# Reordering the start of a fused adaLN, attention and feed-forward kernel: token tiles on one queue, head columns copied earlier, zero matmuls moved, one row task moved

## The chip, the cores and the metric

The kernel runs on one core of one Trainium2 chip. The metric is the device time of one execution in microseconds (us). "Before" is the tuned kernel. In the profile PE is TensorE, PEld its weight loads, DVE is VectorE, ACT is ScalarE, POOL is GpSimd, SP is the sync engine that issues most DMAs. Times within an execution count from the start of the profiled span.

## The reference

One transformer block: layer norm with a conditioning shift and gain, attention over the last 512 positions of a cache, output projection, a second layer norm, and a gated feed-forward part.

```python
mod = (_silu(c) @ w_mod).reshape(c.shape[0], 6, 1, -1)
sa, ca, ga, sb, cb, gb = (mod[:, i] for i in range(6))         # abridged
h = _layernorm(x) * (1 + ca) + sa
x = x + ga * _A_ref(h, A_k_cache, A_v_cache, A_wq, A_wo)       # 32 heads, 4 kv heads, width 128
h = _layernorm(x) * (1 + cb) + sb
x = x + gb * _B_ref(h, B_w_gate, B_w_up, B_w_down)             # silu(x Wg) * (x Wu) @ Wd
```

There are 2048 tokens of width 1024, worked on in four chunks of 512, each of four tiles of 128 tokens.

## The kernel before

A small tracker (`T.op`) emits each instruction and puts a semaphore wait before it for every buffer it reads or writes. `warm(n, b)` issues n matmuls of zeros (128x128 by 128x512) into PSUM bank b; they compute nothing. The parts that matter are the head (the first 30 us), where TensorE waits for data, and one background task.

The head loads the four token tiles on two DMA queues, and SP goes on to the conditioning weights:

```python
for t in range(TPC):
    q = Q_xa[t // 2] if t % 2 else Q_x[t]
    T.op(q, lambda: (A if t % 2 else SP).dma_start(x_res[:, t, :], xf[t * P:(t + 1) * P, :]), writes=[B_x[t]])
```

Then each tile is normalized (statistics on DVE for three tiles, on ACT for the fourth), transposed on TensorE, and, between the transposes, the gain (`mod_ca`) is computed with one-column matmuls:

```python
warm(8, WB)
x_first(0)                       # 8 transposes, wait for DVE's norm(0)
warm(4, WB)
x_first(1)
for k in range(3):
    mod_ca(k)
    warm(1, WB)
x_first(2)
# ... mod_ca(3..7), x_first(3), single zero matmuls between ...
warm(4, WB)
x_mod()                          # gain read from PSUM, hT = transposed x * gain
```

The query projection of the first four heads starts from hT without the shift; the shift's own product (`mod_sa`) is still on its way. It is added later as a bias column for each head (the "bias products", one-column matmuls into bank SCB + 2):

```python
mod_sa(2)
mod_sa(3)
# ... DVE copies the shift out of PSUM; k_turn(0): transposes of the first keys ...
warm(2, SCB + 3)
# 32 one-column bias products for 4 heads
warm(3, SCB + 3)
# ... shift(0..4) on DVE and ACT ...
q_out(0)                         # DVE: query of head 0 + its column, read from PSUM
T.op(DVE, lambda: V.tensor_copy(bq[:, :], psap((SCB + 2) * 512, [[2, LEAD + 1]])), ...)   # columns to SBUF
q_out(2, True)                   # ACT, needs bq
q_out(3, True)
# shift(5..7) on DVE, q_out(1)
```

In the main loop, background tasks are Python generators in a list; each iteration runs one step of the first. `row_task` spreads a row over all partitions: POOL builds diagonal matrices, TensorE multiplies them by ones into bank XB, DVE casts the bank (line 588). Bank XB is also one of the two banks of the output projection, which comes after the last head of each chunk.

```python
if i == 31:
    bg.insert(0, row_task(sc_row, B_scr, sc_bf[:, :], B_sc))
```

The softmax here doesn't subtract the row's maximum and nothing guards it: scores larger than these inputs give would overflow.

## Time and profile before

| | before |
|---|---|
| time, three runs | 1281.66 us median, 1280.07 to 1282.6 |
| span of the profile | 1280.4 us (this execution took 1282.21 us) |
| TensorE on the chain that ended last | 99% |
| all waits of TensorE's matmuls | 7.0 us |
| clock below full after the first release | 3.4 us at half |

The chain line of the page says that everything hangs on TensorE:

```profile
PE 99%; DMA 1%; DVE 0%; ACT 0%; POOL 0%; ACTq 0%; issue 0%; DVEq 0%
```

Since TensorE is the chain, only two things can make the kernel faster without doing less: idle time of TensorE and its clock. The view of the waits, for PE (who waited, for whom: us in total, times, longest), lists its idle time up to its last matmul:

```profile
PE ps L268 <- POOL arena L391: 2.2, 1, 2.2
PE ps L268 <- DVE arena L588: 1.9, 1, 1.9
PE ps L268 <- DVE arena L656: 1.4, 1, 1.4
PE ps L272 <- DVE nsc L409: 0.8, 2, 0.4
PE ps L268 <- DVE arena L470: 0.4, 1, 0.4
PE ps L272 <- DVE arena L409: 0.3, 1, 0.3
```

Line 588 is the cast of the row task; it stands at 155.7 us, inside the output projection. The timeline there (start, duration, instruction, and in brackets the idle time before it with its releaser):

```profile
154.40 0.69 DVE L734 TENSOR_TENSOR tmp<-ps,rowb 128x512 f32<-128x512 f32 x1 [6.00 <-PE ps L268]
155.13 0.69 DVE L736 TENSOR_TENSOR x_res<-tmp,x_res 128x512 bf16<-128x512 f32 x1
155.74 0.68 DVE L588 CAST arena<-ps 128x512 bf16<-128x512 f32 x1
...
156.48 1.68 PE L268 MATMUL ps<-arena 128*128 128x512 bf16 x7 [1.89 <-DVE arena L588]
```

The cast queues behind the two residual operations of the first output block, and the second output block needs the bank that the cast reads.

The table of windows gives the granted clock of TensorE (the number after the five engines' busy times and counts):

```profile
27.00:28.00 1.00, 0.00 (x0) 0.00 (x0) 0.96 (x5) 0.66 (x2) 0.00 (x0) 0.97 1.21 313
28.00:29.00 1.00, 0.91 (x3) 0.36 (x4) 0.76 (x2) 0.61 (x2) 0.00 (x0) 0.50 0.87 195
29.00:30.00 1.00, 1.00 (x4) 0.37 (x3) 0.00 (x0) 0.84 (x1) 0.00 (x0) 0.50 0.71 134
30.00:31.00 1.00, 1.00 (x3) 0.30 (x2) 0.00 (x0) 0.91 (x2) 0.00 (x0) 0.50 0.85 237
31.00:32.00 1.00, 1.00 (x5) 0.45 (x4) 0.00 (x0) 0.30 (x1) 0.00 (x0) 0.82 1.08 386
```

For 3.4 us the clock is at half. And the timeline of PE alone shows pieces of the head (four lines out of some thirty):

```profile
7.24 0.71 PE L272 MATMUL ps<-arena,nsc 128*128 128x128 bf16 x8 [0.40 <-DVE nsc L409]
7.79 1.03 PE L268 MATMUL ps<-arena 128*128 128x512 bf16 x4
...
15.65 3.83 PE L268 MATMUL ps<-arena 128*128 128x512 bf16 x16 [0.43 <-DVE arena L470]
...
28.09 4.36 PE L268 MATMUL ps<-arena 128*128 128x512 bf16 x12 [1.38 <-DVE arena L656]
```

They are the first transposes, the zero matmuls after them, the first query matmul at 15.65 us and the first scores at 28.09 us.

### The profile page before, as it was taken

What the parts mean: (1) busy time and instruction counts of PE and PEld (TensorE: products, weight loads), DVE (VectorE), ACT (ScalarE), POOL (GpSimd) and SP (SyncE); (2) the same over time, 40 slices, a digit from 0 to 9 for tenths busy, and PEclk for the clock granted to TensorE, in tenths of its full rate; (3) what the DMA queues carried; (4) which work ended last, traced back from release to release, by engine and by line L of the source; (5) the groups of instructions that cost most, each with busy time, mean ns of one, the idle gap of its engine ahead of it and who ended that gap; (6) DMA issues with size and microseconds to landing.
All of it is one profiled execution on the core that took longest, in us unless ns stands there. A gap on an engine that the chain in (4) does not pass through costs nothing.

```text
span 1280.4 us, 17849 instructions
## 1 busy us (share of the span) xinstructions
PE 1270.6 (99%) x7651; PEld 645.0 (50%) x7651; DVE 477.3 (37%) x884; ACT 339.8 (27%) x384; POOL 41.8 (3%) x102
## 2 busy tenths in 40 slices
PE   8999999999999999999999999999999999999999
PEld 4565545555455564455554444444444444444444
DVE  3555314765137652265422331233222331221222
ACT  3555303555015551055520111011100111011100
POOL 1011000000000010000000000000000000000000
PEclk9999999999999999999999999999999999999999
DMA  9999402966008841055352974046421654035200
GB/s 317 226 242 239 104 1 50 214 141 158 16 17 171 170 105 42 1 128 112 73 150 68 289 234 132 17 142 170 132 74 39 199 150 132 17 112 168 67 9 25
DMA packets 234830, 155.31 MB, mean 121 GB/s; under 512 B 129024, under 2 KB 220032, under 8 KB 234752
## 3 DMA queue, kind: packets, MB, share of 16 engines
q1 hardware_dynamic: 176208, 94.93, 30.8%
q10 hardware_dynamic: 58544, 59.25, 14.7%
q8 instruction: 60, 0.98, 0.3%
q14 instruction: 18, 0.15, 0.0%
HBM read 119.54 MB, written 4.19 MB: 97 GB/s over the span
## 4 chain that ended last, share of the span: by engine, by line
PE 99%; DMA 1%; DVE 0%; ACT 0%; POOL 0%; ACTq 0%; issue 0%; DVEq 0%
PE ps L268 98%; DMA x_res<-in_A_x_dram 1%; PE ps L272 0%; ACT arena L490 0%; DVE tmp L734 0%; DVE arena L656 0%; DVE arena L661 0%; DVE x_res L736 0%; DVE arena L588 0%; ACTq L305 0%; POOL rstd L499 0%; DVE arena L409 0%; DVE arena L736 0%; DVE arena L470 0%; ACTq L308 0%
## 5 line engine op out<-in xcount | busy, mean ns | idle before, releaser
L268 PE MATMUL ps<-arena 128*128 128x512 bf16 (+1 forms) x7378 | 1265.4, 334 | 5.9 <-POOL arena L391 2.2
L268 PEld LDWEIGHTS ps<-arena 128*128 128x128 bf16 x7378 | 635.9, 98 | 624.7 <-issue 5.2
L694 ACT ACTIVATE arena<-ps 128x1024 bf16<-128x1024 f32 x256 | 261.9, 1023 | 358.4 <-PE ps L268 346.7
L919 ACT ACTIVATE arena<-ps 128x512 bf16<-128x512 f32 x112 | 66.9, 597 | 506.5 <-PE ps L268 506.5
L920 DVE TENSOR_TENSOR arena<-ps,arena 128x512 bf16<-128x512 f32 x112 | 77.5, 692 | 276.2 <-PE ps L268 276.2
L734 DVE TENSOR_TENSOR tmp<-ps,rowb 128x512 f32<-128x512 f32 (+1 forms) x65 | 44.4, 683 | 320.8 <-PE ps L268 320.8
L611 DVE CAST arena<-ps 128x512 bf16<-128x512 f32 x124 | 85.8, 692 | 59.7 <-PE ps L268 59.7
L715 DVE TENSOR_TENSOR arena<-ps,rl 128x512 bf16<-128x512 f32 x128 | 88.5, 691 | 4.7 <-DVE rl L712 0.2
L712 DVE RECIPROCAL rl<-ps 128x4 f32<-128x4 f32 x128 | 23.4, 182 | 120.5 <-PE ps L268 120.5
L398 DVE BATCH_NORM_STATS2 st<-x_res 128x6 f32<-128x512 bf16 x62 | 42.4, 683 | 3.7 <-DMA x_res<-in_A_x_dram 3.6
L403 POOL TENSOR_SCALAR rstd<-mv 128x1 f32<-128x1 f32 x28 | 6.2, 221 | 883.5 <-DVE mv L402 883.5
L565 DVE SCALAR_TENSOR_TENSOR arena<-arena 128x1024 bf16<-128x1024 bf16 x24 | 29.2, 1216 | 0.0
L736 DVE TENSOR_TENSOR arena<-tmp,x_res 128x512 bf16<-128x512 f32 (+1 forms) x33 | 22.3, 676 | 1.1
L736 DVE TENSOR_TENSOR x_res<-tmp,x_res 128x512 bf16<-128x512 f32 x32 | 22.1, 692 | 1.1
L414 DVE TENSOR_SCALAR arena<-arena,gain,mod_bf 128x512 bf16<-128x512 bf16 x56 | 20.4, 406 | 0.0
L409 DVE TENSOR_SCALAR nsc<-x_res,mv,rstd 128x1024 bf16<-128x1024 bf16 x30 | 16.0, 534 | 0.0
L580 POOL TENSOR_SCALAR arena<-arena,c 128x128 bf16<-128x128 bf16 x24 | 14.4, 616 | 46.7 <-PE ps L268 46.4
L405 POOL TENSOR_TENSOR rstd<-rstd,mhalf 128x1 f32<-128x1 f32 x28 | 15.8, 564 | 2.3
L268 PEld LDWEIGHTS ps<-sc_bf,arena 128*128 128x128 bf16 x192 | 7.2, 96 | 3.2
L268 PE MATMUL ps<-sc_bf,arena 128*128 128x1 bf16 x192 | 7.3, 163 | 0.0
L402 DVE BATCH_NORM_AGGREGATE mv<-st 128x2 f32<-128x12 f32 x28 | 5.8, 209 | 1.0
L272 PE MATMUL ps<-arena 128*128 128x128 bf16 x32 | 2.8, 219 | 0.3 <-DVE arena L409 0.3
(54 smaller groups left out, 40.0 us busy)
## 6 DMA issues: line engine op xcount, KB each, us to landing
arena<-in_A_wq_dram SPq DMA_DIRECT2D x31, 1024.0 KB, 5.6
arena<-in_B_w_gate_dram ACTq DMA_DIRECT2D x28, 1024.0 KB, 5.4
arena<-in_B_w_up_dram ACTq DMA_DIRECT2D x28, 1024.0 KB, 8.2
arena<-in_A_wo_dram SPq DMA_DIRECT2D x8, 1024.0 KB, 7.0
arena<-in_B_w_down_dram SPq DMA_DIRECT2D x7, 1024.0 KB, 8.2
out_dram<-arena SPq DMA_DIRECT2D x15, 256.0 KB, 2.0
x_res<-in_A_x_dram SPq DMA_DIRECT2D x3, 1024.0 KB, 6.6
arena<-in_w_mod_dram SPq DMA_DIRECT2D x8, 256.0 KB, 7.1
```

The costliest lines, as they stand in the source:

```text
L268: T.op(PE, lambda: TE.matmul(out_ap, lhsT, rhs, start=start, stop=stop, skip_group_check=skip), reads=reads, writes=[bank_buf])
L398: T.op(DVE, lambda: V.bn_stats(st_[sl][:, hf * 6:hf * 6 + 6], x_res[:, t, hf * 512:hf * 512 + 512]), reads=[B_x[t]], writes=[B_st[sl]])
L414: T.op(DVE, lambda: V.tensor_scalar(dst[:, dt, :], dst[:, dt, :], gain[gi][:, dt:dt + 1], mod_bf[:, ccol + dt:ccol + dt + 1], op0=ALU.mult ...
L565: T.op(DVE, lambda: V.scalar_tensor_tensor(mt[n % 2], mt[n % 2], 1.0, sc_row, op0=ALU.mult, op1=ALU.mult, accum_out=mcol[:, n:n + 1]), rea ...
L611: T.op(DVE, lambda: V.tensor_copy(qT_s[qs], bank(b)), writes=[PB[b], B_qT[qs]])
L694: T.op(ACT, lambda: A.activation(ex_s[es][:, 2 * kp:2 * kp + 2, :], banks2(SCB + 2 * kp), AF.Exp, scale=att_scale), writes=[PB[SCB + 2 * k ...
L712: T.op(DVE, lambda: V.reciprocal(rl[r][:, :].rearrange("p (a b) -> p a b", a=2), psap(PVB * 512 + P, [[512, 2], [130, 2]])), writes=both + ...
L715: T.op(DVE, lambda: V.tensor_tensor(o_s[os_].rearrange("p (a b) d -> p a b d", a=2), psap(PVB * 512, [[512, 2], [130, 2], [1, P]]), rlb, A ...
L734: T.op(DVE, lambda: V.tensor_tensor(tmp[s][:, 0:n], bank(b, n), rowb[ri][:, c0:c0 + n], ALU.mult), reads=[B_row[ri]], writes=[PB[b], B_tmp ...
L736: T.op(DVE, lambda: V.tensor_tensor(dst[:, c0:c0 + n], tmp[s][:, 0:n], x_res[:, t, c0:c0 + n], ALU.add), reads=[B_tmp[s], B_x[t]], writes= ...
L919: T.op(ACT, lambda: A.activation(sg_s[ss], bank(gb), AF.Silu), writes=[PB[gb], B_sg[ss]])
L920: T.op(DVE, lambda: V.tensor_tensor(guT[:, ft, :], bank(ub), sg_s[ss], ALU.mult), reads=[B_sg[ss]], writes=[PB[ub], B_gu[ft]])
```

## The change

Its intent is to cut idle time of TensorE in the head, to keep its clock up with zero matmuls, and to take the row task out of the output projection. The diff, cut to its core:

```diff
-            Q_xa = [dq("q_xa%d" % i, A) for i in range(2)]
             for t in range(TPC):
-                q = Q_xa[t // 2] if t % 2 else Q_x[t]
-                T.op(q, lambda: (A if t % 2 else SP).dma_start(x_res[:, t, :], ...), writes=[B_x[t]])
+                T.op(Q_x[t], lambda: SP.dma_start(x_res[:, t, :], ...), writes=[B_x[t]])
 ...
-                T.op(DVE, lambda: V.tensor_copy(gain_f[:, :], gain[0][:, :]), ...)
+                T.op(ACT, lambda: A.activation(gain_f[:, :], gain[0][:, :], AF.Copy), ...)
 ...
-            warm(8, WB)
+            warm(7, WB)
             x_first(0)
-            warm(4, WB)
+            warm(5, WB)
             x_first(1)
 ...
             mod_sa(2)
+            warm(2, SCB + 3)
             mod_sa(3)
 ...
-            warm(2, SCB + 3)
+            warm(3, SCB + 3)
             # bias products
-            warm(3, SCB + 3)
+            warm(5, SCB + 3)
 ...
             # q_out: head 0 no longer reads its column from PSUM, but from bq as the others do
+            T.op(DVE, lambda: V.tensor_copy(bq[:, :], psap(...)), writes=[PB[SCB + 2], B_bq])
             q_out(0)
-            T.op(DVE, lambda: V.tensor_copy(bq[:, :], psap(...)), writes=[PB[SCB + 2], B_bq])
             q_out(2, True)
 ...
-                if i == 31:
-                    bg.insert(0, row_task(sc_row, B_scr, sc_bf[:, :], B_sc))
+                if i == 17:
+                    bg.append(row_task(sc_row, B_scr, sc_bf[:, :], B_sc))
```

More of the change, by code (lines that the diff above doesn't have):

```diff
@@ L302, in load_x @@
                      writes=B_x[ch * TPC:(ch + 1) * TPC])
-            Q_xa = [dq("q_xa%d" % i, A) for i in range(2)]
             T.op(Q_c, lambda: A.dma_start(c_row[:, :], c.rearrange("o (k p) -> (o k) p", p=P)), writes=[B_cT])
             for t in range(TPC):
-                q = Q_xa[t // 2] if t % 2 else Q_x[t]
-                T.op(q, lambda: (A if t % 2 else SP).dma_start(x_res[:, t, :], xf[t * P:(t + 1) * P, :]), writes=[B_x[t]])
+                T.op(Q_x[t], lambda: SP.dma_start(x_res[:, t, :], xf[t * P:(t + 1) * P, :]), writes=[B_x[t]])
             OFF_WO = 0
@@ L465, in x_mod @@
                 mod_gain(0, 0, DT, B_modc, B_g[0])
-                T.op(DVE, lambda: V.tensor_copy(gain_f[:, :], gain[0][:, :]), reads=[B_g[0]], writes=[B_gf])
+                T.op(ACT, lambda: A.activation(gain_f[:, :], gain[0][:, :], AF.Copy), reads=[B_g[0]], writes=[B_gf])
                 for dt in range(DT):
@@ L659, in q_out @@
             def q_out(h, on_act=False):
-                if h == 0:
-                    T.op(DVE, lambda: V.tensor_scalar(qT_s[h], bank(QB0[h]), bank(SCB + 2, 1, 2 * h), None, op0=ALU.add),
-                         writes=[PB[QB0[h]], PB[SCB + 2], B_qT[h]])
-                elif on_act:
+                if on_act:
                     T.op(ACT, lambda: A.activation(qT_s[h], bank(QB0[h]), AF.Identity, bias=bq[:, h:h + 1]),
@@ L672, in _ @@
             shift(4, True)
+            T.op(DVE, lambda: V.tensor_copy(bq[:, :], psap((SCB + 2) * 512, [[2, LEAD + 1]])), writes=[PB[SCB + 2], B_bq])
             q_out(0)
-            T.op(DVE, lambda: V.tensor_copy(bq[:, :], psap((SCB + 2) * 512, [[2, LEAD + 1]])), writes=[PB[SCB + 2], B_bq])
             q_out(2, True)
```

## The prediction

> **What bounds it.** TensorE. The chain of waits is 99% PE over a span of 1280.4 us. The list of PE's waits holds only 7.0 us in the whole run: 2.2 us for the first memset, 1.9 us for a cast of the row task (DVE, line 588), 1.4 us for the shifts before the first scores, 1.5 us in small waits of the head. Besides, one clock loss: the table of windows shows a granted clock of 0.97 in 27 to 28 us, 0.50 from 28 to 31 us, 0.82 in 31 to 32 us, and 1.00 after. That is about 3.4 us at half speed (the timeline's matmuls start every 0.43 us instead of 0.216), a cost of about 1.7 us. All that can be won lies in some 5 to 8 us.
>
> **Each part, costed.**
>
> 1. Row of conditioning. Its second half now falls behind the first output-projection block (PE idle 154.6 to 156.5 us, behind two residual operations and the cast). Appended behind the second chunk's normalization it should run about iterations 27 to 29, inside the head loop, where the bank is free and DVE has slack: -1.9 us.
>
> 2. Clock gate. PE idles about 1.4 us before 28.09 us, after many one-column matmuls. The Trainium skill, "TensorE: Matmul & The Clock Gate" (Part 1), says the gate halves the clock after an idle window of 3413 ns; the trace agrees in length (3.4 us). Five more zero matmuls (2 before the last shift product, 1 and 2 around the bias products) and a shorter wait should keep the window busy: -1.7 us if it works (75 to 80%); the timed runs of before may not all have it.
>
> 3. Head columns copied first. Before, ACT's query copy of head 2 waits 1.1 us for the column copy, which queues behind head 0's DVE copy (0.76 us); the scores start at 28.09 us when that ACT copy ends. With the 0.16 us column copy first, ACT starts some 0.75 us earlier and the scores some 0.7 us earlier: -0.7 us.
>
> 4. Token tiles on SP. The fourth tile (ACT queue) lands 6.5 us after issue, at 8.2 us; the tiles on SP took about 3 us. It should land near 5.5 us. But PE has its own serial work there: the third transposes can move only from 11.38 to about 10.93 us. So only about -0.45 us reaches PE.
>
> 5. Gain copied on ACT instead of DVE: DVE starts the first multiply 0.17 us earlier: -0.15 us.
>
> 6. Cost of the added zero matmuls: the two before the last shift product delay it (its weights landed before): +0.43 us; the third before the bias products: +0.15 us; the two after fill idle time: 0.
>
> Sum: -1.9 -1.7 -0.7 -0.45 -0.15 +0.6 = -4.3 us. As an expectation with the doubt about the clock: about -4.0 us.
>
> **Predicted time** 1277.4 us, range 1275.3 to 1279.6. Chances: faster by over 2% 0.01, within 2% 0.98, slower by over 2% 0.01.
>
> **What would show it.** The 1.9 us wait on line 588 gone; clock 1.00 all through 25 to 35 us and 0.216 us matmul spacing; the first scores at about 27.3 us (28.1 before); the fourth tile's landing near 5.5 us but the first query matmul at about 15.0 us, not 13 (15.65 before); PE busy time down by about 1.7 us.
>
> **What would make it wrong.** The clock gate still closing, or closing in only some executions of either kernel, as its window runs free: then the gain is nearer 2.5 us. The row task meeting another wait in its new place. The SP queue delaying the conditioning weights (the last landed at about 12.8 us), so that the head waits for them.

## The result, and the profile after

The changed kernel took 1278.87 us in the median of four runs (1277.92, 1278.26, 1279.48, 1279.70); the kernel before took 1281.76 us in the same set (1280.07 to 1282.6). The ratio is 0.9979, with a 95% interval from 0.9962 to 0.9996. A ratio here is the mean time of one kernel's fast runs over that of the other's of the same rounds, so it is not quite the ratio of the medians. By the measure of 2% the two kernels are the same. The span of the profile went from 1280.4 to 1277.9 us; the profiled execution of the changed kernel is the one of 1279.70 us, its slowest.

TensorE's waits in the changed kernel:

```profile
PE ps L268 <- POOL arena L389: 2.2, 1, 2.2
PE ps L272 <- DVE nsc L407: 1.1, 1, 1.1
PE ps L268 <- DVE arena L468: 0.4, 1, 0.4
PE ps L268 <- DVE arena L663: 0.3, 1, 0.3
```

The wait of 1.9 us on the row task's cast is gone, and the wait before the scores fell from 1.4 to 0.3 us. But the wait for DVE's first normalized tile, ahead of the first transposes, is now 1.1 us (0.4 us before). The table of windows no longer shows the clock at half at 28 us:

```profile
28.00:29.00 1.00, 0.90 (x5) 0.19 (x2) 0.82 (x2) 0.65 (x2) 0.00 (x0) 1.00 0.67 149
29.00:30.00 1.00, 0.76 (x4) 0.42 (x5) 1.00 (x5) 0.74 (x3) 0.00 (x0) 1.00 0.61 122
30.00:31.00 1.00, 1.00 (x7) 0.42 (x5) 0.54 (x1) 0.91 (x2) 0.00 (x0) 1.00 0.93 271
```

The same four pieces in the timeline of PE:

```profile
7.51 1.04 PE L272 MATMUL ps<-arena,nsc 128*128 128x128 bf16 x8 [1.10 <-DVE nsc L407]
...
8.34 2.34 PE L268 MATMUL ps<-arena 128*128 128x512 bf16 x5
...
16.77 3.89 PE L268 MATMUL ps<-arena 128*128 128x512 bf16 x16 [0.36 <-DVE arena L468]
...
29.24 2.75 PE L268 MATMUL ps<-arena 128*128 128x512 bf16 x12 [0.35 <-DVE arena L663]
```

Here is a surprise. Five zero matmuls take 2.34 us, where four took 1.03 us before: they ran at half clock, 0.43 us each. The first query matmul starts at 16.77 us, 1.1 us later than before, though I had predicted 0.6 us earlier; the first scores start at 29.24 us, not at 27.3 us as predicted. They then run at full clock: from the scores to the next key transposes are 2.59 us instead of 4.20 us. The trace's record of the clock has its first release at 11.50 us (7.47 us before). The clock column of the windows does not show it: it reads 1.00 from the start, although the zero matmuls at 3 to 6 us take 0.43 us in both kernels. One has to read the spacing of equal matmuls to see the start.

So two profiles stand against each other: before, the clock came up early and fell once; changed, it came up late and never fell. Which of this is the change, and which is luck?

### The profile page after: what moved, and what is told of

It is laid out like the page before. It is cut to its first block, busy times and chain, and to the rows that moved or that the text cites. A ratio compares the mean times of both kernels' runs of the same rounds, so it can differ in the third digit from the quotient of the medians.

```text
span 1277.9 us, 17862 instructions
## 1 busy us (share of the span) xinstructions
PE 1271.0 (99%) x7656; PEld 646.3 (51%) x7656; DVE 477.2 (37%) x883; ACT 340.3 (27%) x385; POOL 42.2 (3%) x102
## 4 chain that ended last, share of the span: by engine, by line
PE 99%; DVE 0%; DMA 0%; ACT 0%; issue 0%; ACTq 0%
PE ps L268 99%; PE ps L272 0%; DMA x_res<-in_A_x_dram 0%; DVE st L396 0%; DVE arena L663 0%; ACT arena L471 0%; DVE arena L468 0%; DVE tmp L730 0%; DVE arena L732 0%; DVE nsc L407 0%; DVE mv L493 0%; DVE gain L448 0%; DVE mod_bf L462 0%; DVE bq L669 0%; ACTq L79 0%
## 5 line engine op out<-in xcount | busy, mean ns | idle before, releaser
L268 PE MATMUL ps<-arena 128*128 128x512 bf16 (+2 forms) x7383 | 1265.7, 334 | 3.0 <-POOL arena L389 2.2
```

Source lines behind the costliest of these rows:

```text
L268: T.op(PE, lambda: TE.matmul(out_ap, lhsT, rhs, start=start, stop=stop, skip_group_check=skip), reads=reads, writes=[bank_buf])
```

## The experiments

Theory A: the clock is decided by how busy TensorE is within windows of fixed length that run free of the kernel's start. The Trainium skill, "TensorE: Matmul & The Clock Gate", Part 1, describes such a window of 3413 ns. The length agrees with the profile before: its record of the clock has the half clock from 27.95 to 31.36 us, 3.41 us, and 20.48 us, six times that, from the first release to the fall. Then both events depend on where the windows happen to lie, and idle time of TensorE makes them likely. Theory B: the late release is a fixed consequence of the edit. The other experiments undo one part each. Times of kernels sent together share the runs of the kernel before: first set 1280.15 us median of nine (one of them above 1281), second set 1280.24 us (four above 1281), third set 1280.09 us (two above 1281). The sets ran on three different chips, but the lowest of each are 1280.05, 1280.08 and 1280.03 us, so the sets can be compared to about 0.1 us; where I compare across sets I say so.

### The changed kernel again (first set)

No edit.

> The changed kernel once more, unedited, for a second profile and more times. Theory A (the clock's first release is decided by how busy TensorE is in a free-running window of about 3.4 us, and the changed kernel leaves TensorE idle 1.1 us before the first transposes, so in some executions the release comes one window late): the release time differs from the 11.5 us of the first profile if the window's phase differs, it lies anywhere in about 5.5 to 12 us, and the times fall in a range of about 1.5 us or more (1277.9 to 1279.7). Theory B (the late release is a fixed consequence of the edit, for instance of the later landing of the first tile): release again at about 11.5 us and times within about 0.5 us of each other. Ratio to before about 0.998 in both.

Measured: 1277.85 us median, 1277.77 to 1277.93 in five runs; ratio 0.998 (0.9968 to 0.9993). The timeline of PE of this execution:

```profile
7.08 0.92 PE L272 MATMUL ps<-arena,nsc 128*128 128x128 bf16 x8 [0.67 <-DVE nsc L407]
7.84 1.24 PE L268 MATMUL ps<-arena 128*128 128x512 bf16 x5
...
14.92 3.89 PE L268 MATMUL ps<-arena 128*128 128x512 bf16 x16 [0.36 <-DVE arena L468]
...
27.39 2.75 PE L268 MATMUL ps<-arena 128*128 128x512 bf16 x12 [0.35 <-DVE arena L663]
```

The same code; the five zero matmuls run at full clock, the first query matmul starts at 14.92 us and the scores at 27.39 us, as predicted (15.0 and 27.3 us). The record of the clock has the release at 7.75 us. So the late release is not fixed by the code. My expectation of a spread of 1.5 us within the set was wrong: all five lie together here. Theory B as I wrote it falls; whether the idle time has a part in it is for the next runs.

### Nine, four and one zero matmuls before the first transposes

```diff
-            warm(7, WB)
+            warm(9, WB)      # a3; a4: warm(4); c0: warm(1)
             x_first(0)
```

> The changed kernel with nine instead of seven zero matmuls before the first transposes, which fills the 1.1 us gap with two cold matmuls of 0.43 us and delays nothing (the transposes wait for the vector engine until 7.5 us). Theory A: the release of the clock comes at 8.1 us or earlier in any phase, the first query matmul at about 15.6 us instead of 16.8 us, and the time falls to about 1277.5 us with a narrower spread. Theory B (phase or tile landing alone, the zero matmuls do not matter): no change against the changed kernel, 1278.9 us, release late as often.

> The changed kernel with four instead of seven zero matmuls before the first transposes: the suspected cost enlarged, TensorE is idle about 2.4 us there. Theory A: release one window late in nearly every phase (11 us or later), all times near or above the slower cluster of the changed kernel, about 1279.6 to 1281 us. Theory B: as the changed kernel, 1278.9 us.

> The changed kernel with one instead of seven zero matmuls before the first transposes, so that TensorE is idle about 3.3 us there, nearly a whole window. Theory A (the release of the clock needs a busy window): released one window late in every execution, zero matmuls of 0.43 us still between the first and second transposes, first query matmul at about 16 us or later (14.9 us in the fast profile of the changed kernel), time 1279.5 us or more in all runs. Theory B: no change, 1277.9 us.

Measured: nine, 1277.88 us (1277.85 to 1277.99, five runs). Four, 1279.58 us median: one run at 1277.78, the others 1279.11 to 1279.86. One (second set), 1279.73 us, 1278.83 to 1280.09 in four runs, released at 11.59 us and with the zero matmuls after the first transposes at half clock:

```profile
7.11 1.04 PE L272 MATMUL ps<-arena,nsc 128*128 128x128 bf16 x8 [3.26 <-DVE nsc L407]
7.94 2.34 PE L268 MATMUL ps<-arena 128*128 128x512 bf16 x5
...
16.56 3.89 PE L268 MATMUL ps<-arena 128*128 128x512 bf16 x16 [0.36 <-DVE arena L468]
```

The dose works: the fewer zero matmuls, the more often the slow group. These zero matmuls delay nothing, since the transposes wait for DVE until about 7.1 us in any case; so what they change is the clock. The profile of the run with four happens to be its one fast execution. That run also shows that the expectation "late in nearly every phase" was a little too strong, and with one, a run at 1278.83 us lies between the groups, where 1279.5 us or more was expected of all. For nine I had expected about 1277.5 us and the first query matmul at 15.6 us; its profile has it at 14.95 us, and its times are those of the changed kernel's early executions (1277.85 us). So the two more zero matmuls gain nothing over these; they only keep the slow group away.

Now the windows themselves. For each profile that records the first release, count 3.41 us back from it, and once more, and ask the table of windows how long TensorE was busy there. The rows of the changed kernel, its second execution and, from a later run (two token tiles on ACT's queue), one that was again released late, in this order (the first number after the comma is PE busy):

```profile
4.67:8.08 3.41, 2.31 (x11) 0.87 (x9) 3.29 (x7) 1.15 (x2) 1.61 (x4) 1.00 0.98 347
```

```profile
4.34:7.75 3.41, 2.74 (x12) 1.12 (x11) 3.27 (x8) 1.15 (x2) 1.71 (x5) 1.00 0.98 330
```

```profile
4.26:7.67 3.41, 2.67 (x12) 0.98 (x10) 3.31 (x7) 0.00 (x0) 1.57 (x4) 1.00 0.94 328
```

The first and the third window ended without a release, which came one window later (11.50 and 11.09 us); the second window ended with the release. All profiles with a record of the release:

| run | PE busy in the last window that did not release | PE busy in the window that did |
|---|---|---|
| before | 1.89 | 3.02 |
| changed | 2.31 (and 2.50 in the one before) | 3.42 |
| changed, again | 2.18 | 2.74 |
| one zero matmul | 1.07 | 3.41 |
| tiles as before | 2.67 | 3.42 |
| six others | | 3.41 to 3.42 |

Every window of 2.74 us or more released the clock, none of 2.67 us or less did. That agrees with one threshold for the release near 2.7 of 3.41 us, about 80% busy. It is a fit to eleven profiles, the two nearest windows are only 0.07 us apart, and the start of the windows is inferred from the release. It would explain why the idle time of 1.1 us matters in some executions and not in others: where a window's end falls into or just after it, the window fails.

Across the four changed kernels with nine zero matmuls (five runs each) no run lies more than 0.31 us above its kernel's best. Of the 24 runs of kernels with seven, six lie 1.2 us or more above the fast group of their kernel (or of the same kernel's other set). The state of an unprofiled run is inferred from its time alone. And no profile with nine shows the bad position of the windows: those with a record released at 5.68 to 6.73 us, where seven were enough too (5.95 us in the run without the added zero matmuls). That nine keep the late release away thus rests on the times.

### The row task alone (first set)

The kernel before with only the last hunk of the diff.

> The kernel before with nothing but the row of conditioning moved (appended at iteration 17 instead of put first at iteration 31). If this term is independent of the head: the 1.9 us wait of TensorE on the cast of line 588 is gone, no other wait appears, and the time is 1.9 to 2.1 us below before (ratio about 0.9985). If the gain is given back elsewhere (rival): the wait is gone but the time is within 0.5 us of before.

Measured: 1278.61 us median (1278.03 to 1279.06), against 1280.15 us: 1.5 us faster, ratio 0.9986 (0.9974 to 0.9999). The wait on line 588 is gone and the row is built from about 96 us on instead. The gain is a little below the expected 1.9 to 2.1 us in the median and 2.0 us from best to best (1280.05 to 1278.03). In the profiled execution TensorE waits 0.5 us for the third transposes (0.3 us in the profile before), because the fourth token tile landed at 8.4 us; that is the next question. This profile also has an idle time before the scores like that of the kernel before:

```profile
PE ps L268 <- DVE arena L656: 1.4, 1, 1.4
```

and yet its clock stays at 1.00: the windows, counted from its release at 6.79 us, cut the gap in two, and the longer part of it leaves a window with 2.46 us of work:

```profile
27.26:30.68 3.42, 2.46 (x12) 1.16 (x13) 1.61 (x5) 3.00 (x4) 0.00 (x0) 1.00 0.81 177
```

In the profile of the kernel before the same gap lies in one window, which has 2.17 us of work, and the clock closes at its end:

```profile
24.54:27.95 3.41, 2.17 (x41) 1.16 (x38) 2.86 (x10) 1.81 (x4) 0.00 (x0) 1.00 1.11 359
```

PE's busy time alone does not decide this, though. In the same profile the wait on line 588 leaves a window, on the same grid, with even less work, and the clock stays at 1.00:

```profile
154.24:157.65 3.41, 1.52 (x11) 0.76 (x10) 1.98 (x3) 0.00 (x0) 0.00 (x0) 1.00 0.00 0
```

What differs is the kind of work: here it is all 512-column matmuls; in the window that closed, these make up about 1.1 us (an estimate: five of 0.216 us), and 32 others are of one column. That one-column matmuls count for little would fit both, but no run tests it, so the cause of the closing stays open.

So the loss of clock that I had read as a property of the kernel before was a property of that execution.

### Without the five added zero matmuls (second set)

```diff
             mod_sa(2)
-            warm(2, SCB + 3)
             mod_sa(3)
-            warm(3, SCB + 3)
+            warm(2, SCB + 3)
             # bias products
-            warm(5, SCB + 3)
+            warm(3, SCB + 3)
```

> The changed kernel without the five added zero matmuls around the shift and bias products (0, 2 and 3 there, as before). Theory 1 (they cost 0.65 us of TensorE's serial work and are needed against the closing of the clock in only some phases of its window): first scores 0.6 us earlier, time 1277.2 us in most runs, with single runs 1.7 us above that where the gate closes. Theory 2 (they are what keeps the clock open): the clock closes at about 27 to 28 us in most runs, time about 1278.9 us.

Measured: 1277.26 us median; 1277.21, 1277.24, 1277.26, 1277.64 and 1278.68 us; ratio 0.9977 (0.9964 to 0.9989). Against the changed kernel in the first set (1277.85 us) that is 0.6 us faster. The clock did not close in the profile. So the zero matmuls between the shift products and before the bias products cost 0.6 us, and here they were not needed. The one run at 1278.68 us has no profile, but the record lists its mean clock as 1.000. A window at half clock would show (0.999 in the profiled run before), so a late release is the likelier reading; since three of the fourteen profiles hold no record of the clock at all, it is not settled.

### The token tiles as before (second and third set)

```diff
             for t in range(TPC):
-                T.op(Q_x[t], lambda: SP.dma_start(...), writes=[B_x[t]])
+                q = Q_xa[t // 2] if t % 2 else Q_x[t]
+                T.op(q, lambda: (A if t % 2 else SP).dma_start(...), writes=[B_x[t]])
```

> The changed kernel with the four token tiles on two queues as before. Theory 1 (the fourth tile's landing sets the third and fourth transposes): fourth tile lands at about 8.2 us, third transposes at 11.4 to 11.5 us, first query matmul 0.7 to 0.9 us later (15.7 us), time 1278.6 us. Theory 2 (TensorE's serial work hides it): time within 0.3 us of the changed kernel, 1277.9 us.

Measured: 1279.34 us median, but 1278.00 twice and 1279.34, 1279.56 and 1279.96: three late releases, one of them in the profile (11.09 us). The median thus tells nothing of the tiles. The run was repeated with nine zero matmuls:

> The changed kernel with nine zero matmuls before the first transposes and the four token tiles on two queues as before, so that the clock's release does not blur the comparison with the run with nine (1277.88 us). Theory 1 (the fourth tile's landing at 8.2 us holds up the third transposes): third transposes at 11.4 us after a wait of about 0.5 us on the vector engine, first query matmul at 15.5 us or later (14.95), time 1278.4 to 1278.7 us. Theory 2 (TensorE's serial work hides most of it, as two runs of 1278.0 us with the tiles as before suggest): 1278.0 us, third transposes within 0.2 us of 10.8 us.

Measured: 1278.08 us median (1277.97 to 1278.28), against 1277.88 us with the tiles on SP (first set): 0.2 us. In the profile the fourth tile took up to 5.9 us from issue to landing, at 7.7 us, and the third transposes started at 10.86 us without a wait. Theory 2 holds: TensorE's serial work hides nearly all of it. When the tile lands after 8.2 us, as in the profile before (8.23 us) and with the row task alone (8.37 us), 0.3 to 0.5 us of wait show. On the SP queue the fourth tile landed at 5.8 to 7.2 us in nine profiles, on ACT's queue at 7.4 to 8.4 us in five. The Trainium skill, "DMA: Bandwidth & Descriptors", "Issuing engines are not separate DMA queues", says that DMAs issued from several engines run on the same DMA engines and interleave. The landings fit that: in the profile before SP begins to issue the weights at 1.65 us and ACT issues the fourth tile at 1.8 us, while on SP's queue the tile (2.1 us) goes ahead of them. That this sharing is the cause was not tested.

### The head columns copied after the first query copy, as before (second set)

```diff
-            T.op(DVE, lambda: V.tensor_copy(bq[:, :], psap(...)), ...)
             q_out(0)             # head 0 reads its column from PSUM again
+            T.op(DVE, lambda: V.tensor_copy(bq[:, :], psap(...)), ...)
```

> The changed kernel with the head columns copied after head 0's query copy, as before. If ACT's query copy of head 2 is what the first scores wait for: scores 0.65 us later, time 1278.5 us, with more idle time of TensorE before them (about 1.0 us instead of 0.35). If the scores wait for something else: within 0.2 us of 1277.9 us.

Measured: 1278.57 us median (1278.50 to 1278.98), against 1277.85 us for the changed kernel (first set): 0.7 us. The wait before the scores is 1.0 us instead of 0.3 us:

```profile
PE ps L268 <- DVE arena L655: 1.0, 1, 1.0
```

The view names a shift on DVE, but the last shift here ends at 28.16 us, after the scores have started at 28.15 us. ACT's query copy of head 2 ends at 28.09 us; in the profile before, it ends at 28.03 us and the scores start at 28.09 us. So ACT's copy, as I had expected, is the one that they wait for: a copy of 0.16 us, put ahead of one of 0.75 us, lets a second engine start earlier.

### The gain copied on DVE, as before (third set)

The second hunk of the diff undone, with nine zero matmuls.

> The changed kernel with nine zero matmuls before the first transposes and the gain copied on the vector engine as before. As predicted blind: 0.15 us slower than with nine alone (1278.0 against 1277.88 us). Rival, read from the two profiles (from the conditioning read to the second group of query matmuls 1.74 us before, 1.73 us after, since ACT's first multiply is what they wait for): no difference, below 0.05 us.

Measured: 1277.88 us (1277.86 to 1277.91), against 1277.88 us with nine alone (first set): nothing. The rival is right. With the copy on ACT the first query matmul starts at 14.95 us, with the copy on DVE at 15.02 us; but the second group of query matmuls waits for ACT's first multiply, and the first scores start at 27.42 and 27.43 us.

### The kernel before with its idle time filled (third set)

```diff
-            warm(8, WB)
+            warm(9, WB)
             x_first(0)
 ...
             # bias products
-            warm(3, SCB + 3)
+            warm(8, SCB + 3)
```

> The kernel before with nothing but more zero matmuls where TensorE is idle: nine instead of eight before the first transposes, eight instead of three after the bias products. If the slower executions of the kernel before (1281 to 1282 us beside 1280.1) are those in which the clock closes on the idle time before the first scores: all five runs at 1280.0 to 1280.3 us, clock 1.00 from 24 to 32 us. If they have another cause: some runs at 1281 to 1282 us again.

Measured: 1280.09 us median, 1280.01 to 1280.38 in five runs, beside nine runs of the kernel before with 1280.09 us median and two above 1281. No run was slow, as expected; but seven of the 27 runs of before in the three sets were above 1281, so five clean runs could be chance (about one in five). The record's mean clock sorts these seven: it is 0.999 in the four at 1281.69 to 1282.08 us, where a half-clock window of 3.4 us is due to give 0.9987, and 1.000 in the three at 1281.03 to 1281.27 us, which may be late releases (not shown). So a closing is recorded in only four of 27, and five runs without one are chance in nearly one case of two. The run proves little. It does show that filling this idle time costs nothing.

### A version that beats both (third set)

Zero matmuls only where TensorE is idle anyway: nine before the first transposes, none between the shift products, two before the bias products and six after.

```diff
-            warm(7, WB)
+            warm(9, WB)
 ...
-            warm(2, SCB + 3)         # before mod_sa(3)
 ...
-            warm(3, SCB + 3)
+            warm(2, SCB + 3)
             # bias products
-            warm(5, SCB + 3)
+            warm(6, SCB + 3)
```

> A version meant to beat both: the changed kernel with nine zero matmuls before the first transposes, none before the last shift product, two before the bias products and six after them, so that zero matmuls stand only where TensorE is idle anyway. Expected: early release of the clock as in the run with nine, first scores at about 26.8 us (27.4 in the fast profile of the changed kernel), clock open throughout, 1277.2 us, all runs within 0.3 us of each other. If the two zero matmuls among the shift products are needed against closing: some runs 1.7 us higher.

Measured: 1277.29 us median, 1277.27 to 1277.31 in five runs; ratio to before 0.9976 (0.9963 to 0.9988). Its waits are the shortest list of all:

```profile
PE ps L268 <- POOL arena L389: 2.2, 1, 2.2
PE ps L272 <- DVE nsc L407: 0.8, 2, 0.5
PE ps L268 <- DVE arena L468: 0.4, 1, 0.4
```

It is 0.6 us faster than the changed kernel's early executions (1277.85 us, first set) and keeps to 0.04 us. All kernels here gave the correct result.

## Why the prediction was right or wrong

The measured 1278.87 us lies within the range (1275.3 to 1279.6), 1.5 us above the number. Point by point, with the clock alike on both sides:

| step | predicted | measured | from |
|---|---|---|---|
| row task | -1.9 | -1.5 (median), -2.0 (best to best) | row task alone |
| head columns first | -0.7 | -0.7 | undone |
| token tiles on SP | -0.45 | -0.2 | undone, with nine zero matmuls |
| gain on ACT | -0.15 | 0.0 | undone, with nine zero matmuls |
| added zero matmuls | +0.6 | +0.6 | undone |
| clock no longer closing | -1.7 | 0 in most runs, about -1.6 where before closes | profiles |
| clock released late | not foreseen | 0 in most runs, +1 to +2 where it happens | profiles, dose |

- The row task and the head columns were right, in mechanism and about in size. The row task is most of the gain: the other steady terms sum to -0.7 + 0.6 - 0.2 = -0.3 us, and the whole is 1280.15 - 1277.85 = 2.3 us in the first set.
- The tiles: I had named the serial work of TensorE as the limit, which is right, but took the fourth tile's landing at 8.2 us from one profile; it lands at 7.4 us in other executions, and then even less of it shows.
- The gain copy: the step "DVE starts the first multiply 0.17 us earlier: -0.15 us" stopped at the first multiply. The next group of matmuls waits for ACT, and nothing is left.
- The clock was the step that was wrong in the sum: "-1.7 us if it works" treated the closing in the one profile as the state of the kernel before. Most runs of before in the later sets (20 of 27) lie at 1280.0 to 1280.4 us, 1 to 2 us below the others, and have nothing there to win; the recorded mean clock shows a closing in four of the 27, and in no run of the changed kernels. I had listed this doubt ("closing in only some executions of either kernel"), but the sum still counted nearly the whole term. Against a run of before that does close, it holds: 1281.69 to 1282.08 us less 1277.85 us is 3.8 to 4.2 us, about the 4.0 expected.
- What I did not foresee at all is the other end of the same mechanism. The change takes one zero matmul away before the first transposes (eight to seven) and with it 0.43 us of work at half clock. The idle time there was 0.40 us in the profile before and 0.67 and 1.10 us in the two of the changed kernel; a part of that is the start of the transposes, which varies from 7.08 to 7.51 us. I had costed only the five added zero matmuls. So the busy time of PE, which I said would fall by 1.7 us, went from 1270.6 to 1271.0 us: half-clock work only changed its place. Two of the four runs (1279.48 and 1279.70 us) lie in the slow group; the profile of one of them shows the late release. That is 1.0 of the 1.5 us between prediction and median (1278.87 less 1277.85 us); the rest is about what the tiles and the gain copy fell short (0.25 and 0.15 us).
- Some luck is in the gain of 2.9 us. Three of the four runs of before lie in its slow group, two of the four of the changed kernel in its own: 2.3 us of steady gain, plus 1.6 us (1281.76 less 1280.15) on the one side, less 1.0 us on the other.

What stays open: what decides the closing, the single slow run without the added zero matmuls, and whether the changed kernel's fill at 25 to 28 us is ever needed now that the wait before the scores is shorter. In no profile with the head columns first did the clock close there.

## What to carry to other kernels

Before costing a change of 0.2%, find out whether the executions of the kernel before form groups: one profile is one execution, and a clock event in it may be in only some of the others. Fill idle time of TensorE with zero matmuls only where it is idle anyway; there they are free and, as the runs with nine, seven, four and one show, keep the clock up, and in the serial path each costs its full 0.22 us. When one small copy on an engine gates work on another, put it ahead of the large ones, and when moving a copy, check the next waiter too and not only the first.

## What the Trainium skill lacked or had wrong

- "TensorE: Matmul & The Clock Gate", Part 1, speaks of a busy window ("~3.4µs sustained") and an idle window without a share that separates them. Here windows with 2.74 us or more of TensorE work in 3.41 us released the clock and those with 2.67 us or less did not.
- The same page, "Why this matters for your kernels", advises no idle gaps above about 3 us. Here a gap of 1.4 us, in a window with 2.17 us of work, much of it one-column matmuls, halved the clock for 3.4 us; in the same profile a gap of 1.9 us, in a window with 1.52 us of 512-column matmuls, did not. Neither the gap nor PE's busy time alone tells them apart.
- The same page, Part 1, says that the window runs free of the kernel's start and that the transition therefore varies by ±500 ns. The runs agree with the first, but the variation is larger: two executions of the same changed kernel released at 7.75 and 11.50 us, and its times differ by about 1.7 us for it.
- The same page, Part 4, says that transposes do not count as busy in the same way. The counts above include them; without them the window that released at 7.75 us would have less work (about 2.07 us) than the one that failed at 7.67 us (about 2.15 us), so here they seem to count. It is one pair, 0.08 us apart, with modelled ends: a hint and no proof.
- No page says that the mean clock of a profile can read 1.00 before the first release: here it did, while equal matmuls took 0.43 us instead of 0.216 us.
